# Loads of q and k in a chunked attention, each asked for as two DMAs of four heads

## The chip, the cores and the metric

The program runs on one core of a Trainium2 chip. The core has a matrix engine (PE, with its weight loads shown apart as PEld), a vector engine (DVE), a scalar engine (ACT), GpSimd (POOL), SyncE (SP), which here only issues transfers, and 16 DMA engines that carry out what SP and ACT issue. The metric is device time in microseconds of one execution. All times in this text are microseconds (us) unless ns is written.

## The reference

Two stages, fp32 throughout. The first is a linear attention with decay over 4 batches, 8 heads, 768 positions of 64 numbers, in blocks of 64 positions; the state `kv_state` runs on from block to block within a batch:

```
for b in range(nb):
    intra = einsum(qb, kb) * Dmask          # scores within the block, faded by distance
    intra = einsum(intra, vb)
    inter = einsum(qb * lam_pow, kv_state)  # what came before
    out[block] = intra + inter
    kv_state = lam_block * kv_state + einsum(kb * rev_pow, vb)
```

The second stage takes the attention's output as x (4 x 768 x 512) and computes `u = x + (x^T U V)^T`, then `u + relu(u @ w_ch1) @ w_ch2`, with a hidden width of 2048.

## The kernel before

**The attention.** Work goes in chunks of 128 positions (two blocks of the reference at once): six chunks a batch, 24 in all, numbered s = 0 to 23 and called steps here. In each step PE turns q and k of the chunk (`turn_parts`, L416, 16 small transposes into the PSUM tile `pqk`), ACT copies the turned q and k out (`qt` and `kt`, L422), PE makes the scores (L463), DVE multiplies them by the mask (L472), PE multiplies the masked scores by v (`intra`, L514, into `px`), adds the new part of the state (`state`, L486) and the product of the faded q with the old state (`inter`, L525, into `px` again), and ACT copies `px` out as a tile `x_nat` (L531). `px` has a single buffer, so the next step's `intra` cannot start until that copy is done. POOL scales k (`ks`, L436) and q (`qs`, L447). From step 7 on, the low-rank mixing of earlier chunks (L618, L630, L675, L689, L690) goes between these, a store of each finished chunk (`u_d`, L646), and the loads of the first two tiles of `w_ch1` (`words`, L149), four parts each.

**The order.** The order of everything in the attention is written out by hand in the list `pieces`; each engine works through its own instructions in that order, the DMA issues among them. An instruction that waits holds up all behind it on its engine.

**The loads.** `load` (L329) fetches q, k or v of one chunk: 128 positions by 8 heads by 64 numbers, 256 KB, in rows of 256 bytes. q has three buffers (`qraw`), k four, v three. `prep` asks for q of step s+3 once step s's transposes are in the program, `next_k` for k of step s+4 at the end of step s, `next_v` for v of step s+3 after `intra` and `state`. Loads of q and k are issued by SP; those of v by ACT, where each stands right ahead of the copy of `x_nat`. At the very start the loads of k for steps 0 and 1 are on ACT and those of v for steps 0 and 1 on SP. `parts(s)` says into how many parts step s is cut: two for step 0, whose q and k are also turned and copied in two halves, one for every other step.

**The semaphores of the transfers.** Each DMA of SP and ACT adds to one of eight semaphores when it has landed. The eight are given out in turn, in the order in which the program places the DMAs, SP's and ACT's together. Before a DMA is issued its engine waits until the DMA that used the same semaphore before it, the eighth before, has landed.

**After the attention** come the two products of the second stage, on PE from about 112 us to the end.

Of the kernel before, what the change touches and what calls it, by code (L numbers as in the profile page):

```python
# [18 lines left out]
def kernel(  # L19
# [30 lines left out]
    B, H, S, D = q.shape  # L50
# [204 lines left out]
    def divided_steps(parts, fetch, engine, apart=False, raw=None):  # L255
# [28 lines left out]
        def third():  # L284
# [3 lines left out]
            )  # L288

        return [load, high, low, third] if apart else [load, split]  # L290

    more_w = []
# [33 lines left out]
    def parts(s):  # L326
        return 2 if s == 0 else 1

    def load(name, s, engine):  # L329
        b, c = divmod(s, NT)  # L330
        t = raw_pool.tile(
            [P, H, D], FP32, tag=f"{name}raw", bufs=4 if name == "k" else 3, name=f"{name}raw"
        )
        source = {"q": q, "k": k, "v": v}[name]
        n = H if name == "v" else H // parts(s)
        for h in range(0, H, n):
            engine.dma_start(
                out=t[:, h : h + n, :],
                in_=source[b, h : h + n, c * P : (c + 1) * P, :].rearrange("h p d -> p h d"),
            )  # L340
        raw[s, name] = t
# [393 lines left out]
    def load_next(name, engine=nc.sync):  # L735
        if waiting[name]:
            load(name, waiting[name].pop(0), engine)
# [670 lines left out]
    for ft in range(EARLY):  # L1408
        n = 6 + 7 * ft
# [84 lines left out]
```

## Time and profile before

| | |
|---|---|
| Time, median of 3 runs | 641.93 us (641.23 to 645.38) |
| The profiled execution's own time | 642.39 us |
| Its span, first to last instruction | 640.6 us |
| PE busy | 631.0 us, 98% |
| PE share of the chain that ended last | 96% |
| Granted clock | 0.999 |
| qraw loads on SP | 23 of 256 KB, 2 of 128 KB |
| kraw loads | on SP 22 of 256 KB; on ACT 2 of 128 KB and 1 of 256 KB |
| vraw loads | on ACT 22, on SP 2, of 256 KB each |

The profile's page gives busy time of each engine, the share in 40 slices, the DMA queues, the chain of work that ended last and the costliest groups. Beside the page, the trace answers what each engine waited for, what one engine did in order of time, and how busy each engine and the DMA engines were in a given stretch. A DMA's issue is shown with its length on the issuing engine; the landing comes later and is told apart. On SP an issue's length can contain a wait.

### The profile page before, as it was taken

The page shows a single profiled execution, that of the slowest core. Times are in us where ns is not written, and L with a number is a line of the kernel's source. Part 1 is how long each engine was busy: PE and PEld are TensorE (multiplying, and loading weights), DVE is VectorE, ACT ScalarE, POOL GpSimd, SP SyncE. Part 2 cuts the span into 40 slices and gives each one's busy share as a digit, 9 for nine tenths or more (in the row PEclk, how much of TensorE's full clock was granted, in tenths as well). Part 3 has the DMA queues.
Part 4 walks back from the last instruction along what each step waited for, and adds up shares of the span by engine and source line. Part 5 has one row for each costly group of instructions (what it writes and reads, how often), then busy time and mean ns, then how long its engine had stood idle before and what let it go on. Part 6 is the DMA issues. An engine that isn't in the chain of part 4 may idle for free.

```text
span 640.6 us, 13612 instructions
## 1 busy us (share of the span) xinstructions
PE 631.0 (98%) x5203; PEld 530.8 (83%) x5203; DVE 459.5 (72%) x731; ACT 335.1 (52%) x614; POOL 146.4 (23%) x124
## 2 busy tenths in 40 slices
PE   9999989999999999999999999999999999999997
PEld 8889989888888888888888878888888888888886
DVE  6766867757878788788678799785574755855854
ACT  3776757445777777877777745232322322323220
POOL 4475968100000000000377600030120300300300
PEclk9999999999999999999999999999999999999999
DMA  9989996347888798765477786463363363543521
GB/s 218 252 205 266 225 245 161 135 171 269 310 288 273 271 322 290 252 208 202 160 258 231 243 310 222 134 226 99 103 227 98 117 205 100 179 140 99 181 83 65
DMA packets 141379, 128.83 MB, mean 201 GB/s; under 512 B 82498, under 2 KB 99394, under 8 KB 141314
## 3 DMA queue, kind: packets, MB, share of 16 engines
q1 hardware_dynamic: 116192, 121.53, 59.3%
q10 hardware_dynamic: 25122, 6.42, 4.4%
q8 instruction: 41, 0.67, 0.4%
q14 instruction: 24, 0.20, 0.1%
HBM read 78.64 MB, written 48.89 MB: 199 GB/s over the span
## 4 chain that ended last, share of the span: by engine, by line
PE 96%; DMA 2%; DVE 1%; issue 1%; ACT 1%; ACTq 0%; DVEq 0%
PE pz L959 25%; PE pz L1336 14%; PE pz L1334 14%; PE pd L1338 13%; PE z L959 4%; PE pss L463 4%; PE px L514 4%; PE p L959 3%; PE pz L889 2%; PE d L959 2%; PE px L525 2%; PE pqk L416 2%; PE c L959 1%; PE pkv L486 1%; PE pd L900 1%; PE pm L618 1%
## 5 line engine op out<-in xcount | busy, mean ns | idle before, releaser
L1318 ACT ACTIVATE m<-rm 128x512 fp32r<-128x512 f32 x96 | 60.6, 632 | 174.4 <-PE pd L1338 134.2
L1319 DVE SCALAR_TENSOR_TENSOR m<-rm,m 128x512 fp32r<-128x512 f32 x96 | 71.6, 747 | 81.7 <-ACT m L1318 81.7
L959 PE MATMUL pz<-u_hl,w 128*128 128x512 f32 x448 | 110.3, 389 | 0.0
L1334 PE MATMUL pz<-w_hl,m 128*128 128x512 f32 x264 | 102.7, 389 | 0.0
L1336 PE MATMUL pz<-w_hl,m 128*128 128x512 f32 x264 | 102.7, 389 | 0.0
L1338 PE MATMUL pd<-w_d,m 128*128 128x512 f32 (+1 forms) x267 | 101.4, 387 | 0.0
L959 PEld LDWEIGHTS pz<-u_hl,w 128*128 128x128 f32 x448 | 84.1, 188 | 17.5
L285 POOL TENSOR_TENSOR w<-w 128x512 fp32r<-128x512 f32 (+1 forms) x28 | 40.2, 1451 | 213.7 <-DVE w L279 194.3
L1320 DVE SCALAR_TENSOR_TENSOR m<-m 128x512 fp32r<-128x512 f32 x96 | 74.8, 779 | 3.0
L1366 POOL TENSOR_TENSOR o<-o,u 128x512 f32<-128x512 f32 x20 | 29.8, 1517 | 198.9 <-DVE o L1362 198.9
L959 PE MATMUL pz<-u_d,w 128*128 128x512 f32 x224 | 59.7, 389 | 0.0
L1338 PEld LDWEIGHTS pd<-w_d,m 128*128 128x128 f32 x267 | 49.8, 188 | 10.3
L1334 PEld LDWEIGHTS pz<-w_hl,m 128*128 128x128 f32 x264 | 49.6, 188 | 10.4
L1336 PEld LDWEIGHTS pz<-w_hl,m 128*128 128x128 f32 x264 | 49.6, 188 | 10.2
L959 PEld LDWEIGHTS pz<-u_d,w 128*128 128x128 f32 x224 | 42.0, 188 | 8.7
L966 ACT ACTIVATE pz<-pz 128x512 f32<-128x512 f32 x60 | 34.9, 581 | 26.6 <-PE pz L959 26.6
L1336 PE MATMUL pz<-w,m 128*128 128x512 f32 x120 | 46.7, 389 | 0.0
L1334 PE MATMUL pz<-w,m 128*128 128x512 f32 x120 | 46.7, 389 | 0.0
L1338 PE MATMUL pd<-w,m 128*128 128x512 f32 x120 | 46.7, 389 | 0.0
L472 DVE TENSOR_TENSOR sm<-pss,mask 128x512 f32<-128x512 f32 x48 | 30.9, 686 | 20.4 <-PE pss L463 20.4
L970 ACT ACTIVATE r<-pz 128x512 f32<-128x512 f32 x60 | 35.7, 596 | 14.2 <-PE pz L959 12.8
L196 DVE SCALAR_TENSOR_TENSOR sc<-words,sc 128x512 uint32<-128x512 uint32 (+2 forms) x34 | 24.7, 726 | 21.0 <-ACT sc L178 21.0
(144 smaller groups left out, 1112.3 us busy)
## 6 DMA issues: line engine op xcount, KB each, us to landing
r_d<-r SPq DMA_DIRECT2D x96, 256.0 KB, 2.9
rm<-r_d SPq DMA_DIRECT2D x96, 256.0 KB, 2.6
words<-in_moe_w_ch_dram SPq DMA_DIRECT2D x30, 512.0 KB, 4.6
wf<-forms_d SPq DMA_DIRECT2D x53, 128.0 KB, 2.8
u_d<-x_nat SPq DMA_DIRECT2D x24, 256.0 KB, 4.1
u<-u_d SPq DMA_DIRECT2D x24, 256.0 KB, 4.6
qraw<-in_q_dram SPq DMA_DIRECT2D x23, 256.0 KB, 4.8
out_dram<-o SPq DMA_DIRECT2D x23, 256.0 KB, 2.0
```

Of the source, the lines that this page charges most:

```text
L285: engine.tensor_tensor(out=st["third"], in0=st["low"].bitcast(FP32), in1=st["hi"].bitcast(FP32), op=ALU.subtract,)
L472: nc.vector.tensor_tensor(out=sm[:, x], in0=pss[:, x], in1=mask[:, x], op=ALU.mult)
L959: nc.tensor.matmul(out=out, lhsT=weights, rhs=moving, start=start and i == 0, stop=i == len(pieces) - 1, skip_group_check=not start,)
L966: nc.scalar.mul(acc, acc, 1.0 + E)
L970: nc.scalar.mul(r, acc, 4096.0)
L1318: nc.scalar.activation(out=m[:, 0], in_=r, func=AF.Relu, scale=NEAR)
L1319: nc.vector.scalar_tensor_tensor(m[:, 1], r, 0.0, hi, ALU.max, ALU.subtract)
L1320: nc.vector.scalar_tensor_tensor(m[:, 2], hi, E, low, ALU.mult, ALU.subtract)
L1334: nc.tensor.matmul(out=pz, lhsT=m[:, 0, cols], rhs=hi, start=first, stop=False)
L1336: nc.tensor.matmul(out=pz, lhsT=m[:, 1, cols], rhs=low, start=False, stop=end)
L1338: nc.tensor.matmul(out=pd[:, part], lhsT=m[:, 2, cols], rhs=third[:, part], start=first, stop=end, skip_group_check=part.stop != C,)
L1366: nc.gpsimd.tensor_tensor(out=o, in0=o, in1=u, op=ALU.add)
```

## The change

The line that sets how many heads one DMA carries no longer asks `parts(s)`: q and k of every step go as two DMAs of four heads (128 KB each). Loads of v stay whole. The cutting of step 0's transposes and copies still goes by `parts(s)`, and nothing else is touched; the order of the program is the same.

```diff
         source = {"q": q, "k": k, "v": v}[name]
-        n = H if name == "v" else H // parts(s)
+        n = H if name == "v" else H // 2
         for h in range(0, H, n):
             engine.dma_start(
                 out=t[:, h : h + n, :],
                 in_=source[b, h : h + n, c * P : (c + 1) * P, :].rearrange("h p d -> p h d"),
             )
```

## The prediction

> **What bounds the kernel now.** First the page's busy times and its chain of work that ended last, to see which engine the end hangs on:
>
> ```profile
> PE 631.0 (98%) x5203; PEld 530.8 (83%) x5203; DVE 459.5 (72%) x731; ACT 335.1 (52%) x614; POOL 146.4 (23%) x124
> ...
> PE 96%; DMA 2%; DVE 1%; issue 1%; ACT 1%; ACTq 0%; DVEq 0%
> ```
>
> PE is 96% of the chain, and the last loads of q and k land at 104 us, so only the attention can change. PE's gaps over 0.15 us after its first instruction add up to 4.2 us, all before 107 us. Next the busy time by stretch (columns: PE, PEld, DVE, ACT, POOL, granted clock, DMA share, GB/s):
>
> ```profile
> 0.00:35.00 35.00, 32.82 (x742) 29.81 (x744) 24.44 (x56) 19.95 (x46) 16.29 (x20) 1.00 1.02 231
> 35.00:70.00 35.00, 33.70 (x924) 31.34 (x918) 21.90 (x42) 24.00 (x56) 24.51 (x26) 1.00 0.92 225
> 70.00:90.00 20.00, 19.09 (x541) 17.75 (x542) 16.01 (x25) 10.88 (x25) 15.75 (x13) 1.00 1.03 257
> ```
>
> From 0 to 35 and 70 to 90 us the DMA engines are about as full as PE (their records overlap, so the share passes 1): whatever is late there is late because of a full queue. The list of waits (total, times, longest) says who pays:
>
> ```profile
> POOL ks L436 <- DMA kraw<-in_k_dram: 3.4, 3, 1.4
> ACT x_nat L531 <- DMA qraw<-in_q_dram: 3.1, 1, 3.1
> ...
> PE pqk L416 <- DMA qraw<-in_q_dram: 0.2, 1, 0.2
> ```
>
> The second line is the one to see: ACT's copy of `x_nat` reads no q. It stood behind a load of v on ACT, which waited for its turn on one of the eight semaphores, last used by a load of q. ACT's timeline shows the place, and what it looks like when ACT isn't held up (start, length, idle before):
>
> ```profile
> 77.89 0.59 ACT L531 COPY x_nat<-px 128x512 f32<-128x512 f32 x1 [1.24 <-DMA u_d<-x_nat]
> ...
> 83.61 0.37 ACTq L337 DMA_DIRECT2D vraw<-in_v_dram  x1
> 84.08 0.59 ACT L531 COPY x_nat<-px 128x512 f32<-128x512 f32 x1 [3.13 <-DMA qraw<-in_q_dram]
> ```
>
> **The change part by part.** It adds 46 DMAs, 45 on SP and one on ACT, and moves no byte more or less.
>
> *The transfers.* The rows stay 256 bytes, 18 ns each in the trace. A DMA ends in a 4-byte packet on each of 16 engines, 9 ns in the trace: 46 x 9 ns = 0.41 us per engine, over 100 us. I take 0, hidden in the 35 to 70 us stretch; 0.4 if not.
>
> *SP.* A q issue that waits for nothing takes 0.38 us; the halves of step 0 took 0.44 and 0.49. So 45 x 0.46 = 20.7 us more of SP, spread over 24 steps, and nothing at all if two halves take what a whole one took. From one k issue to the next (50.55 to 54.91, 4.36 us) SP spends 0.38 + 0.38 + 1.65 + 0.38 = 2.79; 1.57 are free, and 2 x 0.46 = 0.92 fits. Behind SP's issues stand stores of `u_d` and loads of `words`; a q load is asked for three steps ahead of its use (some 12 us) and lands in 4.8. I take 0.
>
> *PE.* The 16 transposes of a step now wait four times, not twice. The start-to-start time over the present wait between q's and k's transposes is 56 ns in the middle, as between pairs without a wait: 0. The first transposes may start on half a load, but 11 of 14 PE gaps over 0.04 us are not on loads of q or k. Those that are: 0.43 and 0.08 in step 0, already in halves, and 0.24 at 16.79.
>
> *The eight semaphores.* Here is the cost. With 5 DMAs a step (q, k, v, `words`, `u_d`) the eighth before was 1.6 steps old; with 7 it is 1.1 steps old. The list of instructions of the changed program names each wait; I put beside it when that transfer landed in the profile of before. Where the landing comes later than the old issue, ACT stands still, with `x_nat` behind the load:
>
> ```
> load of v   issued before   must now wait for             landed   later by
> v2             6.68         v0                              8.47     1.79
> v3            11.71         words of U                     13.35     1.64
> v4            14.88         k4, first half                 17.60     2.72
> v5            19.29         q5, first half                 21.50     2.21
> v6            23.15         q6, first half                 25.50     2.35
> v7            27.10         q7, second half                28.77     1.67
> v18           77.42         u_d of chunk 7                 79.22     1.80
> v19           83.61         u_d of chunk 8                 85.02     1.41
> v20           86.41         words of w_ch1, part 7         88.07     1.66
> ```
>
> All other v loads find theirs landed. A first half lands earlier than the whole, by at most the 0.58 us that half the rows take (32 per engine x 18 ns), so three of these are upper ends.
>
> Who waits for `x_nat`? The next `intra` (L514) needs `px`. Behind v2 stands no such copy: ACT's next is `qt` at 9.40, after 8.47 + 0.37. Behind v3: `x_nat` moves from 12.13 to 13.77 and ends at 14.36; `intra` of step 1 started at 13.70, so PE loses **0.66**. Its 0.24 wait for q at 16.79 is then swallowed, as PE arrives later: net **0.42**. Behind v4 to v7 each `x_nat` ends at most 0.1 us after the shifted `intra` could start: v4's at 17.60 + 0.42 + 0.59 = 18.61 by the upper end against 17.95 + 0.66 = 18.61. So nothing is added: PE's shift has used up part of each delay, and the landings hang on the full queue, not on PE. Behind v18: `x_nat` 77.89 to 79.69, ended at 80.28, `intra` at 79.71: **0.57**, if a gap of 0.91 us at 82.52, in which PE waited for no semaphore, does not swallow it. I take half, 0.3 (ends 0 and 0.57). v19 and v20 then wait no longer than PE's own shift leaves.
>
> **The sum:** 642.39 + 0.42 + 0.3 = **643.1 us**. The profiled execution is 0.46 over the median of the runs; by the median the same terms give 642.7. A measurement of this kernel tells about 1%, 6.4 us, from no change, so this is "no difference".
>
> **The rivals.**
>
> *Splitting helps.* With every wait on a load gone, PE gains at most 0.43 + 0.08 + 0.24 = 0.75: 641.6. For it: halves free ACT's longest stall (3.1 us, v19 behind a whole q). Against: the engines are full, so a second half lands no sooner. The Trainium skill ("Perfetto Trace Analysis", section DMA Optimizations) says that splitting may let work start sooner where DMA engines are generally idle; by the shares of 1.02 and 1.03 above this case lacks that condition. 0.16.
>
> *No slack behind ACT.* ACT's stall reaches PE in full, through `kt` and `qs` too, but a later PE lessens the next stall: the largest of each stretch counts, 2.72 + 1.80 = 4.5: 646.9. For it: ACT goes on without a pause from `x_nat` to `kt` at 77.89 to 80.95. Against: v19's 3.13 us stall in the profile left PE's next `intra` at 85.21, after its other work. 0.14.
>
> *The stalls add up (slower).* If a v load issued late lands late, SP, which waits on its semaphore in turn, issues late too; the queue runs dry and the landings move along with PE. The point from which this holds: a DMA share clearly under 1 in 0 to 35 us. Then all nine count: 12.4 + 4.9 = 17.3, 659.7. For it: the order of the eight couples both queues. Against: SP keeps up to four or five DMAs under way. The Trainium skill ("DMA: Bandwidth & Descriptors", section Anatomy of one DMA) gives about 2 us of fixed time to each DMA; as an estimate, 46 of these in a row would be 92 us. No run here shows that; the first half-load landed 2.36 us after its issue in all, data included. 0.09.
>
> *SP becomes the bound.* All 20.7 us on the path: 663.1. Against: the 1.57 free above. 0.03.
>
> *The change doesn't do what it says.* The list of instructions has the 46 more; 0.
>
> **How the numbers follow.** My forecast has 0.58: the shares above leave that. Its own range is 642.0 to 644.5 (the ends of its terms, the 0.4 of packets and the half us between profile and median). To hold 8 of 10 the whole range reaches to both near rivals: 640.8 to 648.0, which leaves out 0.12 above. Faster by over 1% (under 636) has no mechanism here: 0.02. Slower by over 1% (over 648.8): 0.09 + 0.03 and a little of the third rival, 0.13. Within: 0.85.
>
> **What would show it.** ACT's waits on landings ahead of `x_nat` grow from 5 us to about 12 in 10 to 30 us and 77 to 88 us; PE gets a new gap of some 0.6 us at L514 near 14 us; SP's DMA rows rise to 48 for q and 44 for k, of 128 KB each; PE's busy time stays at 631; the DMA shares stay. I am wrong if the DMA share in 0 to 35 us falls below 0.95, if steps lengthen where the table has no stall (35 to 70 us), or if anything moves after 112 us.

## The result

The changed kernel took 644.70 us (median of 18 executions, 642.75 to 647.97), the kernel before 641.28 us beside it (18 executions, 639.07 to 645.38). The ratio is **1.0048, 95% interval 1.0034 to 1.0061**: by it 3.1 us slower (2.2 to 3.9); the medians themselves lie 3.4 us apart. That is inside the 1% taken as the bound of no difference, and surely not zero. Forecast were 643.1 us and a loss of 0.7 us by the same median.

The two profiled executions hide the loss: 642.39 before and 642.75 after, the fastest of the changed kernel's executions against one above the median of before. The reason can be read from PE's idle times. Between 5 and 140 us, gaps of over 40 ns that a semaphore ended add up to 1.6 us before and 5.1 us after: 3.5 us more, near the 3.1 of the ratio. Gaps in which PE waited for nothing that the profile shows fell from 3.1 to 0.95 us, and the first `intra` began 0.89 us sooner, since v and k of the first steps had landed sooner. Those two are luck of one execution: over all profiles below, the unexplained gaps lie anywhere from 0.95 to 6.6 us, and the first `intra` begins between 9.2 and 10.3 us with whole loads and with halves alike (11.7 in quarters).

### The profile page after: what moved, and what is told of

It reads as the page before. It is cut to its first block, busy times and chain, and to the rows that moved or that the text cites. A ratio compares the mean times of both kernels' runs of the same rounds, so it can differ in the third digit from the quotient of the medians.

```text
span 641.0 us, 13669 instructions
## 1 busy us (share of the span) xinstructions
PE 629.8 (98%) x5203; PEld 529.8 (83%) x5203; DVE 458.8 (72%) x731; ACT 334.1 (52%) x614; POOL 146.8 (23%) x124
## 4 chain that ended last, share of the span: by engine, by line
PE 90%; DMA 4%; ACT 2%; SPq 1%; DVE 1%; issue 1%; POOL 0%; ACTq 0%; DVEq 0%; POOLq 0%
PE pz L959 25%; PE pz L1334 14%; PE pz L1336 14%; PE pd L1338 13%; PE z L959 4%; PE p L959 3%; PE px L514 3%; PE pz L889 2%; PE pss L463 2%; PE d L959 2%; PE c L959 1%; PE px L525 1%; PE pd L900 1%; DMA qraw<-in_q_dram 1%; PE pqk L416 1%; SPq L337 1%
## 5 line engine op out<-in xcount | busy, mean ns | idle before, releaser
L1338 PEld LDWEIGHTS pd<-w_d,m 128*128 128x128 f32 x267 | 49.8, 188 | 10.3
L1336 PEld LDWEIGHTS pz<-w_hl,m 128*128 128x128 f32 x264 | 49.6, 188 | 10.3
L1334 PEld LDWEIGHTS pz<-w_hl,m 128*128 128x128 f32 x264 | 49.5, 188 | 10.2
L970 ACT ACTIVATE r<-pz 128x512 f32<-128x512 f32 x60 | 35.8, 596 | 14.1 <-PE pz L959 12.8
```

What stands on the lines that cost most here:

```text
L970: nc.scalar.mul(r, acc, 4096.0)
L1334: nc.tensor.matmul(out=pz, lhsT=m[:, 0, cols], rhs=hi, start=first, stop=False)
L1336: nc.tensor.matmul(out=pz, lhsT=m[:, 1, cols], rhs=low, start=False, stop=end)
L1338: nc.tensor.matmul(out=pd[:, part], lhsT=m[:, 2, cols], rhs=third[:, part], start=first, stop=end, skip_group_check=part.stop != C,)
```

## The profile after

Busy times and the chain of work that ended last, from the page of the changed kernel:

```profile
PE 629.8 (98%) x5203; PEld 529.8 (83%) x5203; DVE 458.8 (72%) x731; ACT 334.1 (52%) x614; POOL 146.8 (23%) x124
...
PE 90%; DMA 4%; ACT 2%; SPq 1%; DVE 1%; issue 1%; POOL 0%; ACTq 0%; DVEq 0%; POOLq 0%
...
qraw<-in_q_dram SPq DMA_DIRECT2D x48, 128.0 KB, 4.0
```

PE's work is the same; in the chain its share fell from 96% to 90%, and transfers and ACT took its place. The last line shows the 48 half loads of q, which land 4.0 us after their issue (the median; 4.8 for whole ones in the profile before).

Busy time by stretch (columns as before: PE, PEld, DVE, ACT, POOL, granted clock, DMA share, GB/s):

```profile
0.00:35.00 35.00, 31.12 (x718) 28.30 (x720) 23.47 (x55) 18.76 (x43) 16.21 (x20) 1.00 1.02 230
35.00:70.00 35.00, 33.50 (x931) 31.33 (x933) 21.80 (x43) 23.65 (x56) 23.21 (x26) 1.00 0.89 221
70.00:90.00 20.00, 18.71 (x535) 17.51 (x535) 16.07 (x26) 11.50 (x28) 17.50 (x14) 1.00 1.03 259
```

The transfers fill their engines as before; PE lost 1.7 us in the first stretch, 0.2 in the second, 0.4 in the third. The waits say through whom (total, times, longest):

```profile
ACT x_nat L531 <- DMA kraw<-in_k_dram: 4.7, 3, 1.9
...
ACT x_nat L531 <- PE pkv L486: 3.8, 1, 3.8
...
ACT x_nat L531 <- DMA qraw<-in_q_dram: 2.9, 1, 2.9
...
PE pss L463 <- DVE kv L494: 1.3, 2, 0.9
...
ACT x_nat L531 <- DMA u_d<-x_nat: 1.2, 1, 1.2
PE px L514 <- ACT x_nat L531: 1.1, 2, 0.7
...
PE px L514 <- DVE sm L472: 0.9, 1, 0.9
```

ACT's standing ahead of `x_nat` grew as forecast. (The 3.8 put down to PE is the load v3, which waited for words of U.) The names of transfers in these lines are not safe: the view names the last semaphore event ahead of the copy. By the semaphores themselves, ACT stood 12.6 us at its loads of v for the eighth DMA before: for v0 (1.24, at v2), words of U (3.22, v3), v10 (0.44, v11), stores `u_d` (1.30, 0.52, 2.25 and 1.19, at v12, v13, v18 and v19), and for halves of q or k only 2.43 (v4, v5, v23). So 10.2 of the 12.6 us were spent on transfers that the change does not cut; what is new is that they are the eighth before. `PE px <- ACT x_nat` is the wait that was forecast. The two waits of PE on DVE were not, and before had neither.

The forecast gap, in the timeline of ACT and then of PE (start, length, what, idle before):

```profile
13.24 0.43 ACTq L337 DMA_DIRECT2D vraw<-in_v_dram  x1
13.72 0.59 ACT L531 COPY x_nat<-px 128x512 f32<-128x512 f32 x1 [3.77 <-PE pkv L486]
```

```profile
14.36 1.15 PE L514 MATMUL px<-vraw,sm 128*64 128x64 f32 x32 [0.72 <-ACT x_nat L531]
```

`x_nat` at 13.72 (forecast 13.77), `intra` of step 1 at 14.36 (forecast 14.36). And the way that was not forecast, in the timeline of all engines behind v18:

```profile
79.74 0.42 ACTq L337 DMA_DIRECT2D vraw<-in_v_dram  x1
...
80.26 0.59 ACT L531 COPY x_nat<-px 128x512 f32<-128x512 f32 x1 [2.85 <-DMA qraw<-in_q_dram]
...
80.90 1.15 PE L514 MATMUL px<-vraw,sm 128*64 128x64 f32 x32 [0.34 <-ACT x_nat L531]
...
81.71 0.57 ACT L689 ACTIVATE u_hl<-pm 128x512 fp32r<-128x512 f32 x1
...
82.32 0.69 DVE L690 SCALAR_TENSOR_TENSOR u_hl<-u_hl,pm 128x512 fp32r<-128x512 f32 x1 [1.42 <-ACT u_hl L689]
...
82.92 0.68 DVE L630 TENSOR_TENSOR x_nat<-pm,x_nat 128x512 f32<-128x512 f32 x1
...
83.53 0.41 DVE L494 TENSOR_TENSOR kv<-pkv,faded 128x256 f32<-128x256 f32 x1
...
84.09 0.72 PE L463 MATMUL pss<-qt,kt 64*128 64x128 f32 x8 [0.94 <-DVE kv L494]
```

Read it downwards. (The load v18 waited for the store `u_d` of chunk 7, which landed at 79.66; the name `qraw` in the second line is such an unsafe one.) The late load puts back `x_nat`, which costs PE 0.34 us at once. It puts back everything behind `x_nat` on ACT as well, `u_hl` among it. DVE needs `u_hl` and stands 1.42 us; behind it in DVE's order are L630 and the new state `kv`; and PE's scores are held up by `kv` for **0.94 us**: they write into the PSUM bank that held `pkv` (both carry the tag `pss` in the kernel), and `kv` is what reads `pkv` out. The same stall is paid twice, and more dearly the second time.

## The experiments

Every ratio is against the kernel before, run beside it on the same chip. Two readings of each trace are used throughout. **ACT's standing**: at each load of v, the idle time of ACT right ahead of the issue, up to the landing of the eighth DMA before (the last event on its semaphore). **PE's waits**: its gaps of over 40 ns between 5 and 140 us that a semaphore ended.

```
kernel                    DMAs more   ACT's standing   PE's waits   ratio [95%]
before                            0              3.9          1.6   
v_behind_x_nat_whole              0              1.1          3.3   0.9998 [0.9980, 1.0017]
one_row_dmas                     46              5.6          1.5   1.0002 [0.9983, 1.0020]
halves_to_8                      16              8.4          3.2   1.0030 [1.0005, 1.0054]
halves_from_9                    30             10.7          5.2   1.0013 [0.9990, 1.0035]
the change                       46             12.6          5.1   1.0048 [1.0034, 1.0061]
halves_again (the change)        46             12.8          6.1   1.0047 [1.0026, 1.0068]
v_behind_x_nat_halves            46             17.3         11.4   1.0141 [1.0108, 1.0174]
small_dmas                       46             24.7         13.6   1.0184 [1.0156, 1.0213]
quarters                        138             50.9         35.8   1.0599 [1.0570, 1.0628]
```

Both readings are of one execution, the ratio of many; the kernel before and its 0.9998 twin, with 1.6 and 3.3, show how far one execution strays. (By the traces, halves_to_8 has 16 DMAs more and halves_from_9 30, where the expectations say 17 and 29.) The four kernels that are not in the table are told in their sections.

The theory, called A in the expectations: ACT stands at its loads of v for the turn of a semaphore, and what stands behind on ACT reaches PE. The rivals: SP's 45 more issues (B), the transfers themselves (C), and SP's queue, where small transfers come late (D).

### The change again

> The changed kernel once more, for a second profile and a second ratio. Every theory: 1.003 to 1.006 of the kernel before. Theory A (a load of v on ACT waits for the eighth DMA before it and holds the copy of x_nat, which intra waits for): gaps of 0.3 to 0.7 us at L514 that end with x_nat, near 14 us and 81 us, again. Theory B (46 more issues on SP, or the packets that end a DMA, make the transfers slower): no such gap is needed; late landings everywhere. Theory C (the split itself: PE waits for second halves of q and k): gaps at L416 that end with a load of q or k.

646.51 us against 643.52, the same ratio as before. Of the gaps that A expected, those near 14 us were small (0.23 us at 14.35, 0.20 at 18.53, both behind `x_nat`), and none came near 81 us; two of 0.91 and 0.92 us came by way of DVE (23.63 and 57.20 us). The largest gaps were elsewhere (list of waits, then the window from 70 to 90 us):

```profile
PE pm L618 <- DMA vp<-vp: 2.3, 2, 1.5
```

```profile
70.00:90.00 20.00, 17.75 (x455) 16.73 (x452) 12.72 (x25) 11.26 (x28) 15.77 (x13) 0.91 0.90 226
```

The mix at L618 waited for small transfers of `vp`, issued at 66.67 to 69.71 us and landed by 73.15: up to 4.5 us each, where before took 2.2 to 3.2 us. Right behind these gaps the granted clock fell to 0.91 of full speed in this stretch, which is taken up at the end. So the places differ from one execution to the next while the sum is alike. Of the 6.1 us of PE's waits here, 2.25 are `vp`'s: in this execution D is about as large as what came through ACT.

### Loads of v behind the copies of qt and kt

```diff
         step += [("prep", s + 1)] * more
+        step += [("next_v", s - 1)] * (s > 0)
...
-        step += (both if s > NT else both[::-1]) + [("next_v", s), ("inter", s)]
+        step += (both if s > NT else both[::-1]) + [("inter", s)]
```

Whole loads:

> The kernel before with the same move of the loads of v, q and k whole. Theory A: the 4.9 us that ACT stood ahead of x_nat go, of which PE had lost little: 0.996 to 1.000. B and C say nothing of it beyond 0.998 to 1.002. The distance between this and the same move with halves is what B and C are worth: A says under 0.001, B and C 0.004.

Halves:

> The changed kernel, but each load of v is asked for one step later, behind the copies of qt and kt, so that no copy of x_nat stands behind it on ACT. Same number of DMAs. Theory A: the loss goes, 0.997 to 1.001 of the kernel before, and no gap at L514 ends with x_nat. B and C: the loss stays, 1.003 to 1.006.

1.0084 [1.0054, 1.0115] whole and 1.0081 [1.0051, 1.0110] in halves. The move costs 0.8% by itself, so it does not give back what the change lost, as A had it. With the loads of v so late, the 46 more DMAs cost nothing on top by these ratios, although ACT's standing rose from 0 to 16.1 us: here it lies behind the copies. That speaks against B and C, though weakly: the difference of the two ratios is known to some 0.4%, nearly as much as the loss in question, and PE's waits in the two profiles are 4.2 and 8.2 us. What the 0.8% is was not settled; the profiled execution of the whole version waits for q at 13.57 us (2.19 us) and for `vp` at 73.92 us (1.10 us).

### Whole loads and small DMAs

Beside whole loads, one more DMA of 128 rows of one number behind each load of q and k from step 1 on, into a tile that nothing reads:

```diff
+        if name != "v" and s > 0:
+            i = 2 * s + (name == "k")
+            engine.dma_start(out=pad[:, i : i + 1], in_=source[b, 0, c * P : (c + 1) * P, 0:1])
```

> The kernel before with q and k whole, but behind each load of q and k of steps 1 to 23 a further DMA of one number for each of 128 rows, into a tile that nobody reads: as many DMAs on SP and as many turns of the eight semaphores as in the changed kernel, no load split. Theory A: the v loads wait as in the changed kernel or a little longer, since whole loads land later than first halves: 1.003 to 1.008. B: 1.003 to 1.006. C: 0.999 to 1.001.

1.0184, four times the loss of the change, beyond what was expected. The waits (lines are 4 higher in this kernel: L535 is the copy of `x_nat`):

```profile
ACT x_nat L535 <- DMA pad<-in_q_dram: 4.6, 2, 2.3
ACT x_nat L535 <- DMA vraw<-in_v_dram: 4.1, 2, 2.6
ACT x_nat L535 <- DMA pad<-in_k_dram: 3.7, 1, 3.7
```

ACT stood for the landing of the small DMAs (by the semaphores 7.7 of its 24.7 us; the names in the lines are as unsafe as above) and for other transfers. This alone could be their number or their rows; one_row_dmas below tells these apart.

### Halves in the first nine steps, and in the rest

```diff
-        n = H if name == "v" else H // 2
+        n = H if name == "v" else H // 2 if s < 9 else H
```

> Halves for the loads of steps 0 to 8 alone (17 more q/k DMAs than before, all asked for before about 40 us); steps 9 to 23 whole. My theory A (ACT stands at its loads of v for the turn of a semaphore, and x_nat behind it makes the next intra late): the five stalls of v3 to v7 are all here, so the 0.66 us of step 1 and the joins behind it at 23 us stay: 1.2 to 1.9 us, ratio 1.002 to 1.003, and the second part gives little. Rival D (the queue behind SP: the small transfers of vp, u_d and words stand behind more loads and land late, about 70 us on): the loss is in the other part, and this one gives 0 to 0.6 us, 1.000 to 1.001.

```diff
+        n = H if name == "v" else H // 2 if s == 0 or s >= 9 else H
```

> Whole loads up to step 8, halves from step 9 on (29 more DMAs). A: v18 to v20 alone are left, 0.3 to 1.2 us, 1.0005 to 1.002. D: nearly all of the loss of the full change, 2 to 3 us, 1.003 to 1.005, with PE gaps at the mix (L618) on vp near 70 us. If the two parts together give clearly less than 1.0048, the stalls feed one another.

1.0030 and 1.0013: together 1.0043. So the loss seems spread, and most of it by the middle values is in the part where the forecast put six of its nine stalls (the intervals overlap, and that of the second part reaches below 1). In both profiles the forecast places stand out. Of halves_to_8, ACT, its wait, and PE:

```profile
14.49 0.37 ACTq L337 DMA_DIRECT2D vraw<-in_v_dram  x1
14.91 0.58 ACT L531 COPY x_nat<-px 128x512 f32<-128x512 f32 x1 [5.34 <-DMA words<-in_moe_U_dram]
```

```profile
15.54 0.69 PE L514 MATMUL px<-vraw,sm 128*64 128x64 f32 x8 [2.13 <-ACT x_nat L531]
```

Of halves_from_9:

```profile
81.94 0.39 ACTq L337 DMA_DIRECT2D vraw<-in_v_dram  x1
82.43 0.58 ACT L531 COPY x_nat<-px 128x512 f32<-128x512 f32 x1 [4.70 <-DMA qraw<-in_q_dram]
```

```profile
83.07 1.19 PE L514 MATMUL px<-vraw,sm 128*64 128x64 f32 x32 [2.18 <-ACT x_nat L531]
```

It is v3 behind the words of U and `intra` of step 1, as forecast, and v18 behind a store `u_d` (landed 81.87; not the q of the line) and `intra` of step 16, as forecast. Only the size is not 0.66 and 0.57 but 2.13 and 2.18 us, since in these executions the awaited transfer landed later (v3 could go at 14.49, not at 13.24). A is seen at work; D's late `vp` is in neither list of PE's waits. (The profile of halves_to_8 is of the slowest of its twelve executions, 651.23 us: besides the gap shown, two stretches at half clock and a gap of 2.49 us at 93.81 that the profile doesn't explain.)

### Loads of v asked for by SP

```diff
-        load_next("v", nc.scalar)
+        load_next("v")
```

The same was done to the one load of v that `third_v` asks for, so all 24 are on SP. Whole loads:

> The kernel before with the loads of v asked for by SP in place of ACT, at the same place of the program. ACT then stands before no load of v, so x_nat never waits behind one. A: 641 to 644 us beside 642 of before (0.998 to 1.003): the 3.1 us stall of v19 goes, but SP has one more load per step that it may hold back for a turn of a semaphore. D: slower, 1.003 to 1.008, since the queue of SP is where things wait.

Halves:

> The changed kernel with the loads of v asked for by SP. A: without ACT's stalls the halves cost nothing any more: the same as the run with whole loads on SP within 0.2%. D: the halves cost here too, 0.4 to 0.6% over the run with whole loads on SP, or more, since all seven loads of a step now stand in one queue.

1.0150 [1.0112, 1.0188] whole, 1.0213 [1.0179, 1.0246] in halves. ACT stands at no load of v now, and still the halves cost 0.6% more: A in its narrow form, ACT alone, fails here. The waits of the version with halves show where SP's standing comes out:

```profile
PE pm L618 <- DMA vp<-vp: 6.8, 4, 3.6
...
PE px L514 <- issue: 6.3, 3, 3.4
...
PE pqk L416 <- DMA kraw<-in_k_dram: 2.1, 3, 1.4
```

(With whole loads the first is 3.0 and the second 4.3. The second is time for which the profile shows no cause.) Whichever engine has to wait before an issue, what stands behind it there comes late: on ACT its copies, on SP the spreading of `vp` and the next loads. So D is real where SP is that full. In the changed kernel SP carries 22 loads fewer than here.

### Loads of v right behind x_nat

```diff
-        step += (both if s > NT else both[::-1]) + [("next_v", s), ("inter", s)]
+        step += (both if s > NT else both[::-1]) + [("inter", s), ("next_v", s)]
```

Whole loads:

> The kernel before with each load of v issued by ACT right behind the copy of x_nat of its step in place of right ahead of it; nothing else moves. A stall of ACT for the turn of a semaphore then stands ahead of faded, qt and kt, not of x_nat. If waiting ahead of x_nat is what counts (A): 0.996 to 1.002 of before. If ACT has no slack anywhere (the stall only meets the next join, kt and the scores): 1.003 to 1.008, like the run with the load behind kt.

Halves:

> The same move in the changed kernel. A: within 0.2% of the run with whole loads, and no PE gap at L514 ended by x_nat behind a load of v. If the cost comes by SP's queue or the split itself: 0.4 to 0.6% over the run with whole loads, as without the move.

0.9998 whole, 1.0141 in halves. With whole loads the place is as good as the old one. With halves, ACT stands for 17.3 us and PE pays more than before the move; that no other copy would mind, as A had it, is wrong. PE's waits in this trace:

```profile
PE pss L463 <- ACT kt L422: 5.2, 3, 3.5
PE pss L463 <- DVE kv L494: 4.9, 3, 2.5
```

The gaps left L514 and `x_nat`, and came up at the scores, half behind `kt` and half behind DVE's `kv`. Moving what stands behind the waiting load moved the gap along. That speaks for the standing as the cause, and here no copy of ACT's could take it. `kv` is again the second way seen at 84.09 us above.

### As many DMAs, of one row each

```diff
+        if name != "v" and s > 0:
+            i = 2 * s + (name == "k")
+            engine.dma_start(out=pad[:, i, :], in_=source[b, 0, c * P : c * P + 1, 0:8])
```

> The kernel before, all loads whole, plus one DMA of a single row of 32 bytes behind each load of q and k of steps 1 to 23, into a tile that nothing reads: 46 DMAs more, as in the change, with next to no bytes and one row in place of 512. If the number of DMAs is what costs (turns of the eight semaphores and SP's issues): 1.003 to 1.007. If cutting the transfers is what costs (later or uneven landings of halves): 1.000 to 1.001.

**1.0002 [0.9983, 1.0020]**: 46 more DMAs, on the same queues as in the change, cost nothing. So neither SP's 45 issues nor the number of DMAs in the turn of the semaphores is the price. By the expectation this result meant that the cutting of the transfers costs; the list of turns, read afterwards, offers another reading. What differs is which DMA each load of v must wait for. In the change and here alike seven DMAs are asked for per step, but in the list of instructions the loads of v stand up to four places earlier here. By the two lists:

```
load of v   the change: waits for     here: waits for
v3          words of U                v1
v4          k4, first half            k3
v5          q5, first half            q4
v6          q6, first half            a one-row DMA
v7          q7, second half           k6
```

v1, k3, q4 and k6 landed, in the profile of before, 0.45 to 1.15 us ahead of the end of the issue in question; the change's five land 1.23 to 2.35 us behind it. ACT's waits for transfers ahead of `x_nat`, here:

```profile
ACT x_nat L535 <- DMA qraw<-in_q_dram: 2.1, 1, 2.1
ACT x_nat L535 <- DMA kraw<-in_k_dram: 1.6, 1, 1.6
ACT x_nat L535 <- DMA vraw<-in_v_dram: 1.4, 1, 1.4
```

5.1 us, as in before (3.1 + 1.2 + 0.6 = 4.9). Hardly more standing, no time more. This run alone does not tell the turns from the cutting, since no load is cut here either. The change's traces do: 10.2 of its 12.6 us of standing were for transfers that were not cut (8.0 of 12.8 in halves_again), and these took no longer to land than before (medians up to 110 us: `u_d` 4.0 and 4.1 us after 4.3 before, v on ACT 4.0 and 4.5 after 4.4). That answers C: the transfers were not slower, ACT waited for younger ones. The run also explains small_dmas, which puts its DMAs in the same places: the two differ in the rows of each DMA alone, 128 of four bytes or one of 32, so its 1.8% are the 128 rows. Such a DMA lands 5.2 us after its issue, and the whole loads of q beside them 5.3 instead of 4.8 (medians).

### Quarters

```diff
+        n = H if name == "v" else H // 2 if s == 0 else H // 4
```

> Loads of q and k from step 1 on in four DMAs of two heads each: 138 DMAs more than before, 92 more than the change; 13 DMAs a step, so that a load of v waits for a transfer asked for in its own step or the last one. A: every step stalls ACT until a part of a load lands that was asked for 2 to 4 us ahead: 1.02 to 1.04. SP's issues alone (138 x 0.46 = 63 us, of which 24 x 1.6 = 38 us free): 1.01 to 1.04 as well, with SP busy without a break. If only the few tight places count: 1.005 to 1.01.

681.60 us, 1.0599: above the highest of the ranges. Of the waits, the two that matter, then the first stretch:

```profile
ACT x_nat L531 <- DMA kraw<-in_k_dram: 34.7, 10, 5.7
...
PE px L514 <- ACT x_nat L531: 16.8, 9, 3.6
```

```profile
0.00:35.00 35.00, 27.19 (x556) 24.35 (x556) 19.07 (x47) 13.38 (x33) 11.21 (x16) 1.00 0.75 170
```

With 13 DMAs a step, a load of v waits for a part of a load of k that was asked for in its own step or the last; ACT stands 50.9 us, PE waits 35.8 us, and the DMA share falls to 0.75: loads of v that are issued late leave the DMA engines dry. This is the third rival of the prediction (the stalls add up) with its own sign, a share clearly under 1; what SP's 138 issues add to it was not told apart. The change did not reach that point; this kernel did.

## Why the prediction was right, and where it was not

**Right: the class and the mechanism.** The result lies in the range, within 1%, as given with 0.85, though 0.2 us above the forecast's own range of 642.0 to 644.5: it was the width left for the rivals that held. The stall of ACT for the turn of a semaphore is the main cause: it grew from 3.9 to 12.6 us (forecast: 5 to about 12). Through it PE waited 3.25 of its 5.1 us (at 14.36, 23.03, 55.82, 80.90 and 84.09 us). Where it first reaches PE the forecast held to 0.05 us (13.72, 14.36). That closeness is luck: the same gap was 0.23 us in halves_again and 2.13 in halves_to_8. Of the table's nine loads six stood (v2 to v5, v18, v19); v11 to v13 and v23 stood without being in it. The prices of nothing held as far as they were tested: 46 issues cost nothing (one_row_dmas; its DMAs end in one 4-byte packet each, not in sixteen, so the 0.4 us for packets stayed untested), PE's busy time stayed, 0.24 us of waiting at 16.79 were swallowed, and nothing moved in the second stage (its first product started at 115.58 instead of 115.33 us).

**Right: the two terms.** The first was priced at 0.66 ahead of the swallowed 0.24 and measured 0.72; the second was taken at 0.3 (ends 0 and 0.57) and measured 0.34, the half of a term taken for want of a better value.

**Wrong: the sum of 0.7 us, where 3.1 were measured.** The step that failed is "Who waits for `x_nat`? The next `intra` (L514) needs `px`." It followed the stall out of ACT by one way, `x_nat` to `px`. ACT has others, through DVE. From the trace after:

- "Behind v4 to v7 each `x_nat` ends at most 0.1 us after the shifted `intra` could start", and "so nothing is added": v4 stood 1.45 us. Behind its `x_nat` on ACT stood the two operations that begin to cut the words of U (`sc`, L177 and L178); DVE waited for them, and `sm` behind it came late: PE idle 0.90 us.

```profile
20.18 0.46 ACT L178 ACTIVATE sc<-sc,vp 128x192 uint32<-128x192 f32 x1
...
20.67 1.22 DVE L196 SCALAR_TENSOR_TENSOR sc<-words,sc 128x192 uint32<-128x192 uint32 x1 [1.37 <-ACT sc L178]
...
23.03 0.47 PE L514 MATMUL px<-vraw,sm 128*64 128x64 f32 x9 [0.90 <-DVE sm L472]
```

- "All other v loads find theirs landed": by the table's own measure, against the start of the old issue, two did not. The store `u_d` that v12 now waits for landed at 50.04 before, and v12 was issued at 49.76; for v13 it was 54.45 against 54.08. Only against the end of these issues were 0.1 us and nothing left. With all of it shifted, v12 stood 1.30 us (and v13 0.52); by `u_hl` and `kv`, PE was idle for 0.35 us at 55.82. In halves_again the same place cost 0.92 us.
- "v18 ... I take half": besides the 0.34, the 0.94 by `u_hl` and `kv` at 84.09.

These three, 2.2 us, with 0.53 us for the second half of q of step 2 at 12.43 and 0.23 for `vp` at 98.50, are the missing part of PE's 3.5 us. The term that was mis-sized is thus the stall's reach: taken at 0.7 us, it measured 3.25 in the trace after.

**Which rival was nearest.** *No slack behind ACT* asked for 4.5 us. ACT's standing grew by 8.7 us and PE's waits by 3.5, a share of 0.40; the share was 0.73 in the two runs with more of it ((11.4 - 1.6) / (17.3 - 3.9) behind `x_nat`, (35.8 - 1.6) / (50.9 - 3.9) in quarters). The truth lies between forecast and that rival, whose 0.14 was too little. *Splitting helps* did not come, and the engines stayed full: the condition that the Trainium skill names ("Perfetto Trace Analysis", section DMA Optimizations), engines that are generally idle, was not met after the change either (a share of 1.02). *SP the bound* falls with one_row_dmas. The 92 us of fixed time taken one after another fall with the change itself, 3.1 us slower; and the figure is for another path, since the section of the Trainium skill cited there ("DMA: Bandwidth & Descriptors", section Anatomy of one DMA) describes transfers issued by GpSimd.

**The signs.** "Steps lengthen where the table has no stall" came true (55.82 us, and 57.20 in halves_again), and it is the sign that the sum was too small. The share in 0 to 35 us stayed above 0.95 (1.02, and 0.97 in halves_again).

**Left open.** How the late small transfers of `vp` in halves_again hang on the halves, and what the 0.8% of the loads of v behind `kt` are. Each of the three moves that took the loads of v away from ahead of `x_nat` brought a cost of its own with halves, and none gave the loss back; so that the standing is the cause rests on the traces, on one_row_dmas, where the standing grew by only 1.7 us and the time not at all, and on the two rising together. No version here beats the kernel before.

## What to carry to other kernels

Cutting a transfer shifts which earlier transfer every later issue has to wait for; the count of DMAs was free here, the wrong turn was not. So list, for each issue on an engine that also computes, which landing it waits for and with what margin, and treat margins under a microsecond as none. Then follow the stall out of that engine by all of its later instructions to the end of a step, not by the next one alone.

## What was not expected of the hardware

**A PE gap can cost more than its length.** In the 14 profiles of this study the granted clock is recorded from 8 to 14 us on; it is 1.00 or 0.50, and changes on a grid of 3.41 us. There are 18 stretches at half clock before the end, of one grid window or two. All 15 windows with 1.97 us of PE idle time or more were followed by one; of 11 windows with 1.5 to 1.8 us three were; none with less was, unless the clock was already halved. So the point lies near half a window. A window at half clock costs up to 3.41 / 2 = 1.7 us of matmul time: in halves_again 2.25 us of gaps at 70.05 to 73.47 us brought half clock from 73.47 to 76.88. The Trainium skill ("TensorE: Matmul & The Clock Gate", section Part 1: The HAM clock gate) has the window of about 3.4 us and the half clock, and lets it fall after at least one idle window. By these traces less is enough: a window that was idle for 58% of its length (1.97 of 3.41 us) always was.

For the change this is the smaller part of the loss. Averaged over all executions, 0.19% of full clock was missing (30 executions) against 0.085% in the kernel before (71): 0.1% of 643 us, some 0.7 us. In the comparison of halves_again, the executions with a mean clock of 0.999 or more alone have medians of 645.74 (5 of 12) and 642.79 (19 of 25), still 2.95 us apart.

**128 rows of four bytes are dear, one row is free.** 46 DMAs of 128 such rows cost 1.8% (small_dmas), 46 of one row of 32 bytes nothing (one_row_dmas), in the same places of the same queues. The 128 rows are 512 bytes in all, and a DMA of them took 5.2 us to land beside full queues.
